# An adaLN block's forward and backward pass on one core: x in front of w_mod, the tail's loads and stores in a written order, and three filter gradients at a stage seam

## The chip, the core and the metric

The kernel runs on one core of a Trainium2 chip. The metric is the device time of one execution in microseconds. Three runs of the kernel before took 1512.26, 1512.44 and 1514.15; their median is 1512.44. The engines are named as in the profile: PE multiplies matrices (PEld loads its weights), DVE and ACT work on vectors, POOL and SP issue DMAs here, and POOL also does a few small vector operations. An engine executes its instructions in the order in which they stand in the program; PE, DVE, ACT, POOL and SP wait for each other through semaphores.

## What is computed

The reference is one block and its gradients. x is [1, 2048, 576], c is [1, 576], and the outputs are the block's result and eight gradients:

```
mod = (silu(c) @ w_mod).reshape(1, 6, 1, 576)        # sa, ca, ga, sb, cb, gb
h = layernorm(x) * (1 + ca) + sa
x = x + ga * irfft2(rfft2(h) * (w_r + 1j * w_i))     # spectral filter, 2048 x 576
h = layernorm(x) * (1 + cb) + sb
x = x + gb * ((h @ w_gate) * (h @ w_up) @ w_down)    # hidden width 4608
# returned: x, and the gradients of A_x, w_r, w_i, w_gate, w_up, w_down, c, w_mod
```

out_0 is the result, out_1 the gradient of x, out_2 and out_3 those of the filter (w_r, w_i), out_4 to out_6 those of the three big matrices, out_7 and out_8 those of c and w_mod.

## The kernel before

Rows are split into 16 tiles of 128 rows. The transforms are matmuls with tables of cosines and sines, made in steps over the 16 tiles and over 9 planes of frequencies (a plane and its mirror image are done as a pair, so there are 8 pairs). Three parts matter here.

**The head** (lines 330 to 640). SP issues the loads in a written order: c, a table, tile 0 of x (`x_load(0, 1)`, line 447), one section of w_mod (`mod_load(MGB)`), tiles 1 to 3 of x, four tiles of grad_out (gonA), w_down, tiles 4 to 7 of x, and so on. For each tile of x, `s1_stats` makes mean and variance on DVE (line 184) and ACT their root (186), `s1_norm` the normalized tile n1r (line 521, ACT, or 523, DVE), and `turn16` a first transform of it on PE into PSUM (line 200), which ACT copies out (203). `gate()` (line 504) multiplies the section of w_mod with silu(c) on PE and copies the result from PSUM to gbT on DVE (lines 512 and 516). `go_turn` transposes a tile of grad_out on PE (532) and scales it by gbT on DVE (533). Groups of the matmul u4 (576), which need four such tiles, are put between. A scheduler places the instructions of each engine by priority; `in_order` adds edges that fix an order on one engine.

**The middle** (lines 640 to 960) is one long PE-bound stretch over 36 blocks of the hidden width, from about 110 to 1235 us.

**The tail** (from line 960) is done in three stages and an end. Stage 1 (steps `t1_norm`, `t1_out`, `t1_turn`, one tile each, four steps deep) does the second layernorm's backward pass and stores gx1_d by POOL (line 1217). Stage 2 (`t2_cols`, `t2_rows`, `t2_filter`, `t2_back`, one pair of planes each) transforms and multiplies by the filter; `t2_more` makes the filter's gradients with `filter_grad(g)` (four DVE instructions, lines 1325 to 1327, and a load of Xn), those of even g one per step, and those of g = 3, 5 and 7 in the steps 4, 6 and 8. Stage 3 (`t3_cols`, `t3_rows`, `t3_norm`, `t3_sums`, one tile sa each) transforms back and does the first layernorm's backward pass: `t3_rows` multiplies on PE into one bank with the tag csB (line 282), ACT copies half of it to ye (284), and DVE folds both into ghr (285, 286) and so frees the bank; `t3_norm` loads gxc, makes gn (1426), w with its sum (1044), ab (1046) and u (1047), and in five tiles one more filter gradient; `t3_sums` makes ob (1052) in one of two buffers, and POOL stores it to out_1 (1464). POOL also halves two columns of the filter gradients (`scale_ends`, 1418), stores them in pieces of three planes (1439), and, at sa = 7, the mirrored planes to a scratch tensor gback_d (1443), from which SP copies them turned to out_2 and out_3 at the end (1531). At sa = 7 also four of the five loads of rows of w_mod's last four sections are issued (`section_load`), which `section_sum` (1157) sums on DVE at sa = 9, 10, 12, 13 and 14.

Beneath the three stages PE does the forward matmul of the block's second half as fill: 32 outputs n3, each of 36 matmuls u3p (line 1503), whose left operand comes in chunks `hl` of nine blocks through six slots, `hlt[0]` to `hlt[5]`, that lie over memory of earlier tiles; ACT copies a finished output (1508), DVE adds it to x1 (1516, 1517), and POOL stores it (1522). The first four chunks and the pieces of w_down are issued by POOL between the stores of gx1_d (`queued_load`), the later ones by SP. `deal` writes the order of PE, ACT and DVE for the whole tail by hand: so many fills to a step of each stage (24, 24, 26), then, at the end, 12 fills, a spread of dca (the gradient's row sums) on PE (1135), 12 fills, the spread of dsar, 80 fills, the last reduction gcp (1554), and the rest. Around the spreads ACT writes ten rows o8 of out_8 (1148); DVE sums five last sections, and makes gcd (1548) for gcp.

```
q = (0, 24, 24, 26)[stage]                       # line 1063
q = q * at // steps - q * (at - 1) // steps
...
hl = hlt[(0, 2, 3, 1, 4)[slot[0]] if slot[0] < 5 else (0, 2, 3, 5, 1, 4)[(slot[0] + 1) % 6]].tile(...)
...
if k in (4, 6, 8):
    filter_grad(k - 1)
```

The last tile pair takes its odd outputs (n3 = 29 and 31) in two banks, csA and csB, that hold sums of stage 3 before; csA is free once DVE has read dca and dsa from it (1121, 1127).

Of the kernel before, what the change touches and what calls it, by code (L numbers as in the profile page):

```python
# [19 lines left out]
NT = 16  # L20
# [66 lines left out]
def build(ctx, tc, A_x, A_w_r, A_w_i, B_w_gate, B_w_up, B_w_down, c_in, w_mod, grad_out,  # L87
# [240 lines left out]
    with ExitStack() as hs:  # L328
# [91 lines left out]
        def x_load(t0, t1):  # L420
            nc.sync.dma_start(h2p[:, t0:t1, 0:D], x_v[:, t0:t1, :])
# [23 lines left out]
        wms = {}  # L445
        T = {"F16": load_table(hp1, "F16")}
        x_load(0, 1)
        wms[MGB] = mod_load(MGB)
        x_load(1, 4)
        go_load(0)  # L450
        wd_load(0)
        x_load(4, 8)
# [129 lines left out]
        def u4_groups(n, eng=None):  # L582
            for _ in range(n):
                u4_group(u4_done[0], eng)
                u4_done[0] += 1

        gate()
        s1_norm(0)
        go_turn(0)
        s1_stats(1)  # L590
        s1_stats(2)
        for t in range(1, NT):
            if t in (3, 5, 7, 10):
                s1_stats({3: 4, 5: 6, 7: 8, 10: 12}[t])
            s1_norm(t)
            go_turn(t)
            if t == 1:
                pe_turn(0)
                wd_load(2)
                wms[MSB] = mod_load(MSB, True)  # L600
            if t == 2:
                mod_make(MGB, wms[MGB], "a")
                wms[MCB] = mod_load(MCB)
                for c, filt in enumerate((wr_v, wi_v)):
                    nc.sync.dma_start(back_d[c].rearrange("k j f -> j k f"), turned_rows(filt))
                nc.gpsimd.memset(wn[:, :, :, DF:FP], 0.0)
                for c, filt in enumerate((wr_v, wi_v)):
                    nc.sync.dma_start(wn[:, c, 0:NPR + 1, 0:DF], filt[:, 0:NPR + 1, :])
                    nc.sync.dma_start(wn[:, c, NPR + 1:NT, 0:DF], back_d[c])
                for k_ in ("GB", "I16"):  # L610
                    T[k_] = load_table(hp1, k_)
            if t == 3:
                pe_turn(1)
            if t == 7:
                scaled_table()
                mod_make(MCA, wms[MCA])
            if t == 11:
                shift_row()
                mod_make(MGA, wms[MGA], "a")
            if t == 14:  # L620
                mod_make(MSB, wms[MSB], "a")
            u4_groups({4: 2, 5: 1, 6: 1, 8: 2, 9: 1, 10: 1, 12: 2, 13: 1, 14: 1}.get(t, 0))
# [351 lines left out]
    with ExitStack() as ts:  # L974
# [79 lines left out]
        def deal(held, proj, ends):  # L1054
            made, s2, w2 = scaled["made"], scaled["2"], scaled["w2"]
            more, seq, acts = held + proj, list(lead), made[0:2] + s2[0:1] + w2[0:1] + made[2:3] + s2[1:2] + w2[1:2] + s2[2:3]
            dves, ofs = list(ends["sums"]), []
            for n, (stage, k, ins, own_a, own_v) in enumerate(staged):
                last_ = len(seq)
                seq += ins  # L1060
                steps = sum(x[:2] == (stage, k) for x in staged)
                at = sum(x[:2] == (stage, k) for x in staged[:n + 1])
                q = (0, 24, 24, 26)[stage]
                q = q * at // steps - q * (at - 1) // steps
                fills, more = more[:q], more[q:]
                seq += fills
                fill = [then_act[i_.name] for i_ in fills if i_.name in then_act]
                if stage == 1:
                    own = [then_act[i_.name] for i_ in ins if i_.name in then_act]
                    acts += own + s2[k + 1:k + 2] * (at == max(1, steps - 2) and k > 1) + (w2[k:k + 1] + made[k + 1:k + 2]) * (at == 1 and k > 1) + fill  # L1070
                else:
                    acts += own_a + fill
                    if at == 1:
                        now, ofs = ofs, []
                        if stage == 3:
                            dves += [i_ for nm, s_ in (("gn", 2), ("stt", 2), ("ob", 3), ("ab", 2), ("res", 2), ("fold", 1), ("unit", 2), ("sec", 2)) for i_ in ends["own"].get((nm, k - s_), [])]
                    if stage == 2:
                        dves += own_v
                    if at == steps:
                        dves += now  # L1080
                for i_ in fills:
                    ofs += then_dve.get(i_.name, [])
            dves += ofs + ends["dve"]
            sections, ofs = ends["sections"], []
            for at, ins, act in ends["pe"]:
                fills, more = more[:at], more[at:]
                seq += fills + ins
                acts += [then_act[i_.name] for i_ in fills if i_.name in then_act] + act
                ofs += [then_dve[i_.name] for i_ in fills if i_.name in then_dve]
            ofs += [then_dve[i_.name] for i_ in more if i_.name in then_dve]  # L1090
            cuts = (0, 2, 4, len(sections))
            for a, b, of in zip(cuts, cuts[1:], ([[]] * 3 + ofs)[-3:]):
                dves += sections[a:b] + of
            in_order(seq + more)
            in_order(acts)
            in_order(dves)
# [185 lines left out]
        def hl_load(nq, eng=nc.sync, behind_=None):  # L1282
            if nq >= 30:
                hl = new_wm()[:].rearrange("p (a b) -> p a b", b=256)
            else:
                slot[0] += 1
                hl = hlt[(0, 2, 3, 1, 4)[slot[0]] if slot[0] < 5 else (0, 2, 3, 5, 1, 4)[(slot[0] + 1) % 6]].tile([128, 9, 256], BF, name="hl")
            hl = hl if nq >= 30 else hl[:]
            queued(eng, behind_, hl, hhT_d[nq // 4, :, 9 * (nq % 4):9 * (nq % 4) + 9, :])
            if nq == 13:  # L1290
                in_order([last[eng], ld3["gxc", "ins", 0]])
            return hl
# [8 lines left out]
            return hl  # L1301

        first_hl = []
        for t, *loads in ((1, (0, 7), 0, (7, 7), (14, 7)), (2, 1), (3, (21, 7)), (4, 2), (5, (28, 7), (35, 1)), (6, 3)):
            for x in loads:
                if isinstance(x, int):
                    first_hl.append(queued_load(t, hl_load, x, nc.gpsimd))
# [21 lines left out]
        with ExitStack() as r2:  # L1329
# [18 lines left out]
            def t2_more(k):  # L1348
                if 1 < k < NPR + 2:
                    filter_grad(2 * pairs[k - 2])  # L1350
                if k in (4, 6, 8):
                    filter_grad(k - 1)
                if k in (1, 2):
                    spread((dcb, dga)[k - 1])
                if k == 2:
# [27 lines left out]

            def t2_back(n):
                plane_back(T["GB"], sds[n % 2], pairs[n], nrest, utB, new)

            pipeline(NPR, [t2_cols, t2_rows, t2_filter, t2_back], 2)
        T["IF"] = load_table(tl0, "IF", "tA", nc.gpsimd)
# [20 lines left out]
        def t3_rows(sa):  # L1409
            ye, *own["fold", sa] = rows_back(zzs[sa], [ps_fp.tile([128, 512], FP32, name="yp", tag="fp"), ps_cs.tile([128, 512], FP32, name="yp", tag="csB")], T["I16"][:], c3, ghr3[:, sa % 3, :])  # L1410
            own["ye", sa] = [ye]
            nc.sync.dma_start(xcs[sa % 3][:], x_v[:, sa, :])
            nc.scalar.activation(out=part(n1cs[sa % 3][:]), in_=part(xcs[sa % 3][:]), func=ACT.Identity, bias=nmr1g[:, sa:sa + 1], scale=rstd1g[:, sa:sa + 1])

        def scale_ends(s0, s1):
# [4 lines left out]
        def t3_norm(sa):  # L1420
# [15 lines left out]
                scale_ends(0, NPR + 1)  # L1436
            if sa > 3 and sa % 2 == 0:
                c, a = sa // 2 % 2, 3 * (sa // 4 - 1)
                nc.gpsimd.dma_start((o2_v, o3_v)[c][:, a:a + 3, :], wn[:, c, a:a + 3, 0:DF])
            if sa == 7:  # L1440
                scale_ends(NPR + 1, NT)
                for c in range(2):
                    nc.gpsimd.dma_start(gback_d[c], wn[:, c, NPR + 1:NT, 0:DF])
                rG.close()
                T["wm"] = pool("wme", 4)
                wmE.extend(section_load(m, MGA, 4, new_wm()) for m in range(4))
            if sa in (9, 10, 12, 13, 14):
                mark = traced()
                section_sum(len(own_e), wmE[len(own_e)][0], early, 4, 0)
                if not own_e:  # L1450
                    wmE.append(section_load(4, MGA, 4, new_wm()))
                own_e.append(sa)
                own["sec", sa] = of_engine(mark, "DVE")

        units, wmE, own_e = {0: 1, 1: 9, 3: 11, 4: 13, 6: 15}, [], []

# [3 lines left out]
        def t3_sums(sa):  # L1460
            ob = c3.tile([128, D], BF, name="ob1")
            ld3["last"] = norm_end(*ld3.pop(sa), n1cs[sa % 3][:], ob[:], "1").ins
            own["ob", sa] = [ld3["last"]]
            nc.gpsimd.dma_start(o1_v[:, sa, :], ob[:])
            if sa == 0:
                add_zero(csD, csE)
            diag(csD, csE, 0, ghr3[:, sa % 3, :], n1cs[sa % 3][:], DS, DC + 1, sa == NT - 1)

        pipeline(NT, [t3_cols, t3_rows, t3_norm, t3_sums], 3)
        mark = traced()  # L1470
        diag_rows(dca, csD, csE, 0, DC + 1)
        dsa = diag_sums(tl, csD, csE, 0, "dsa")
# [8 lines left out]
        for tp_ in range(NT // 2):  # L1481
# [10 lines left out]
            for group in [[(0, 0), (1, 0)], [(0, 1), (1, 1)]] if tp_ == 0 else [[(0, 0)], [(0, 1)], [(1, 0)], [(1, 1)]]:  # L1492
                mark = traced()
                p2 = {}
                for ti, h in group:
                    n3 = 4 * tp_ + 2 * ti + h
                    p2[ti] = ps_cs.tile([128, 512], FP32, name="u3q", tag="cs" + "AB"[n3 // 2 % 2]) if tp_ == NT // 2 - 1 and n3 % 2 else ps_u3.tile([128, 512], FP32, name="u3p")
                    if h == 0:
                        obs[ti] = o2p.tile([128, D], BF, name="ob3", bufs=3)
                mms = {}  # L1500
# [51 lines left out]
        for m0, w in ((0, 4), (4, 1)):  # L1552
# [3 lines left out]
                nc.scalar.copy(gcr[0:1, 0:512], pp[0:1, 0:512])  # L1556
            else:
                nc.vector.tensor_copy(gcr[0:1, 512:576], pp[0:1, 64:128])
        end_pe.append((80, pe_since(mark), of_engine(mark, "Activation")))
        nc.sync.dma_start(out_7[0:1, :], gcr[0:1, :])  # L1560
        in_order(end_sp)
        deal(held, proj, dict(sums=sums_dve, own=own, dve=end_dve, sections=sections, pe=end_pe))
# [58 lines left out]
```

## Time and profile before

| what | value |
|---|---|
| median of 3 runs | 1512.44 us (1512.26 to 1514.15) |
| the profiled execution | 1509.32 us |
| its span, first to last instruction | 1507.5 us |
| mean granted PE clock | 0.989 |
| PE idle, 0 to 20 us and 20 to 40 us | 7.6 and 1.8 us |
| PE idle, 1245 to 1305 us | 5.9 us |
| PE busy, 1355 to 1385 us | 23.8 of 30 us |
| PE busy, 1435 to 1455 us | 13.7 of 20 us |
| DVE busy, 1335 to 1385 us | 49.0 of 50 us |
| DMA share, 1325 to 1345 us; 1405 to 1465 us | 0.18 to 0.19; 0.91 to 1.09 |

The span runs from the first to the last instruction of one profiled execution; what the device time has more lies around it. A wait is given as the engine and line that waited, the engine or DMA that ended the wait, the total, how often, and the longest. In a timeline each row is a start, a duration, the engine, the line, the instruction with output<-inputs, and in brackets how long the engine stood idle before it and what ended that. Where the engine named had long been done, a DMA is the likelier cause.

### The profile page before, as it was taken

What the parts mean: (1) busy time and instruction counts of PE and PEld (TensorE: products, weight loads), DVE (VectorE), ACT (ScalarE), POOL (GpSimd) and SP (SyncE); (2) the same over time, 40 slices, a digit from 0 to 9 for tenths busy, and PEclk for the clock granted to TensorE, in tenths of its full rate; (3) what the DMA queues carried; (4) which work ended last, traced back from release to release, by engine and by line L of the source; (5) the groups of instructions that cost most, each with busy time, mean ns of one, the idle gap of its engine ahead of it and who ended that gap; (6) DMA issues with size and microseconds to landing.
All of it is one profiled execution on the core that took longest, in us unless ns stands there. A gap on an engine that the chain in (4) does not pass through costs nothing.

```text
span 1507.5 us, 27854 instructions
## 1 busy us (share of the span) xinstructions
PE 1460.3 (97%) x10713; PEld 987.2 (65%) x10713; DVE 1045.1 (69%) x2533; ACT 571.3 (38%) x1212; POOL 232.4 (15%) x368
## 2 busy tenths in 40 slices
PE   7999999999999999999999999999999998998986
PEld 5665544666666666666766766666666677776764
DVE  7485754666777776776766776677767667498876
ACT  6666733222222222222222222222222237575664
POOL 1101211110110110110211111111111122211311
PEclk8999999999999999999999999999999999999998
DMA  9867985888777778776876775876967769854894
GB/s 320 255 189 204 245 235 147 177 161 164 143 148 157 147 149 151 147 166 133 158 155 133 165 163 122 169 154 130 167 146 141 132 144 347 310 172 148 243 265 128
DMA packets 474404, 268.61 MB, mean 178 GB/s; under 512 B 397597, under 2 KB 444702, under 8 KB 473886
## 3 DMA queue, kind: packets, MB, share of 16 engines
q1 hardware_dynamic: 447246, 168.67, 52.5%
q0 software_dynamic: 27024, 98.16, 22.6%
q8 instruction: 84, 1.38, 0.4%
q14 instruction: 50, 0.41, 0.1%
HBM read 104.99 MB, written 78.89 MB: 122 GB/s over the span
## 4 chain that ended last, share of the span: by engine, by line
PE 83%; DVE 5%; DMA 4%; issue 4%; SPq 1%; ACT 1%; POOL 1%; POOLq 0%; DVEq 0%; ACTq 0%
PE u57p L785 26%; PE u8p L907 18%; PE gup L868 16%; PE u4p L576 9%; PE u3p L1503 3%; PE gup L863 3%; DMA out_dram<-ob 1%; PE fq L649 1%; DMA out_dram<-so 1%; DMA hl<-hhT_d 1%; DVE gwt L1325 1%; SPq L846 1%; PE fq L212 1%; PE fq L276 1%; PE fq L256 1%
## 5 line engine op out<-in xcount | busy, mean ns | idle before, releaser
L912 DVE TENSOR_TENSOR acc<-acc,u8p 128x288 f32<-128x288 f32 (+1 forms) x1088 | 483.0, 453 | 277.5 <-PE u8p L907 273.6
L907 PE MATMUL u8p<-wT,ggT 128*128 128x288 bf16 x1152 | 328.4, 287 | 1.5 <-DVE acc L912 1.4
L907 PE MATMUL u8p<-wT,guT 128*128 128x288 bf16 x1152 | 328.0, 286 | 0.0
L868 PE MATMUL gup<-h2T,wgu 128*128 128x512 bf16 x1152 | 297.9, 380 | 0.0
L787 ACT CAST so<-u57p 128x288 bf16<-128x288 f32 x208 | 82.7, 398 | 508.7 <-PE u57p L785 495.1
L785 PE MATMUL u57p<-h2p,gu_sf 128*128 128x288 bf16 x1088 | 176.7, 286 | 0.0
L785 PE MATMUL u57p<-h2p,gg_sf 128*128 128x288 bf16 x1088 | 176.7, 286 | 0.0
L868 PEld LDWEIGHTS <-wgu 128*128 128x128 bf16 x1152 | 109.6, 98 | 98.9 <-issue 18.1
L907 PEld LDWEIGHTS <-ggT 128*128 128x128 bf16 x1152 | 112.6, 98 | 66.5 <-issue 14.0
L576 PE MATMUL u4p<-goT,wdT 128*128 128x512 bf16 x668 | 154.6, 380 | 0.8 <-ACT ghh_st L172 0.8
L1503 PE MATMUL u3p<-wd,hl 128*128 128x288 bf16 x1044 | 147.0, 292 | 7.5 <-DMA hl<-hhT_d 4.5
L907 PEld LDWEIGHTS <-guT 128*128 128x128 bf16 x1152 | 112.7, 98 | 57.1 <-issue 2.0
L870 ACT CAST gT<-gup 128x512 bf16<-128x512 f32 x144 | 84.3, 585 | 131.4 <-PE gup L868 129.5
L1503 PEld LDWEIGHTS <-hl 128*128 128x128 bf16 x1080 | 105.4, 99 | 41.9 <-DMA hl<-hhT_d 6.0
L785 PEld LDWEIGHTS <-hh_sf 128*128 128x128 bf16 x1152 | 112.7, 98 | 28.4
L785 PEld LDWEIGHTS <-gu_sf 128*128 128x128 bf16 x1088 | 106.4, 98 | 27.0
L785 PEld LDWEIGHTS <-gg_sf 128*128 128x128 bf16 x1088 | 106.4, 98 | 26.8
L870 ACT CAST uT<-gup 128x512 bf16<-128x512 f32 x144 | 84.3, 585 | 77.9 <-PE gup L868 77.0
L576 PEld LDWEIGHTS <-wdT 128*128 128x128 bf16 x668 | 63.6, 98 | 72.2 <-issue 6.5
L785 PE MATMUL u57p<-gonC,hh_sf 128*128 128x288 bf16 x576 | 99.7, 286 | 0.0
L883 POOL DMA_DIRECT2D hhT_d<-hhT x36 | 33.2, 922 | 376.0 <-DVE hhT L872 352.9
L172 ACT CAST ghh_st<-u4p 128x512 bf16<-128x512 f32 x102 | 58.3, 585 | 59.7 <-PE u4p L576 57.9
(277 smaller groups left out, 1719.1 us busy)
## 6 DMA issues: line engine op xcount, KB each, us to landing
hhT_d<-hhT POOLq DMA_DIRECT2D x36, 512.0 KB, 6.4
ghhT_d<-ghh_st POOLq DMA_DIRECT2D x35, 512.0 KB, 4.1
ghh<-ghhT_d POOLq DMA_DIRECT2D x35, 512.0 KB, 7.8
hl<-hhT_d SPq DMA_DIRECT2D x26, 576.0 KB, 6.6
out_dram<-woT SPq DMA_DIRECT2D x68, 128.0 KB, 2.0
wd<-in_B_w_down_dram POOLq DMA_DIRECT2D x37, 144.0 KB, 4.1
wdn<-in_B_w_down_dram SPq DMA_DIRECT2D x18, 288.0 KB, 5.3
out_dram<-so SPq DMA_DIRECT2D x36, 144.0 KB, 2.9
```

What stands on the lines that cost most here:

```text
L172: nc.scalar.copy(dst, src)
L212: nc.tensor.matmul(p_[:, 0:FP], lhsT=G[:, k, pl, :], rhs=z, start=(n == 0), stop=(n == 1))
L576: nc.tensor.matmul(pt[:], lhsT=wdTs[k][:, j, m, :], rhs=goT[:, 4 * sb4:4 * sb4 + 4, m, :], start=(m == 0 and n == 5), stop=(m == n - 1))
L785: mm = nc.tensor.matmul(pw[0][:, 0:288], lhsT=sf[:, t, :], rhs=rhs_n(t, h * 288, 288), start=(t == 0), stop=(t == NT - 1))
L787: followed(mm, nc.scalar.copy(so[:, h * 288:(h + 1) * 288], pw[0][:, 0:288]))
L863: nc.tensor.matmul(pts[-1][:], lhsT=wgu[r, 8, jw * 128:(jw + 1) * 128], rhs=h2T[r, 4 * sb4:4 * sb4 + 4, 4, :], start=True, stop=False)
L868: nc.tensor.matmul(pts[k][:], lhsT=wgu[:, 4 * wi_ + m, jw * 128:(jw + 1) * 128], rhs=h2T[:, ts_, m, :], start=False, stop=(m == 3))
L870: nc.scalar.copy((gT, uT)[wi_][:, th_, :], pts[k][:])
L883: nc.gpsimd.dma_start(hhT_d[:, :, fb, :].rearrange("tp f x -> f tp x"), hhT[:].rearrange("f (tp ti) p -> f tp (ti p)", ti=2))
L907: nc.tensor.matmul(pu[:, 0:288], lhsT=l_, rhs=r_, start=(k == 0), stop=(k == len(mms) - 1))
L912: summed[t] = nc.vector.tensor_tensor(out=ghb(t)[:, hs_] if fbs[-1] == NFB - 1 else dst, in0=dst, in1=pu[:, 0:288], op=ADD).ins
L1503: mms[ti] = nc.tensor.matmul(p2[ti][:, 0:288], lhsT=hls[fb // 9][:, fb % 9, ti * 128:(ti + 1) * 128], rhs=w[:, fb - f0, h * 288:(h + 1) * ...
```

## The change

It has five parts. In the head, tile 1 of x is loaded before the section of w_mod, and an edge is written from the last of `gate()`'s DVE copies to the first DVE instruction of the statistics of tiles 4 and 5. In the first stage of the tail, the slots 2 and 3 of hl change places, and chunks 1 and 2 are queued behind stores 3 and 5 of gx1_d rather than 2 and 4. The filter gradients of g = 3, 5 and 7 move from the steps 4, 6 and 8 of stage 2 to behind the last `t2_back`. In stage 3 POOL's stores of filter gradients are each put behind a given ob store, gback_d is stored in two halves at sa = 9 and 13, and the five loads of w_mod are issued one per tile from sa = 7 to 11, each behind a given load of x (xc 11 to xc 15); a stage-3 step has 25 fills for 26. At the end only n3 = 31 takes a bank of the sums, and 100 fills stand ahead of gcp for 80.

```diff
         x_load(0, 1)
+        x_load(1, 2)
         wms[MGB] = mod_load(MGB)
-        x_load(1, 4)
+        x_load(2, 4)
...
+        mark = traced()
         gate()
+        gate_dve = on_dve(mark)[-1]
...
             if t in (3, 5, 7, 10):
+                mark = traced()
                 s1_stats({3: 4, 5: 6, 7: 8, 10: 12}[t])
+                if t == 3:
+                    in_order([gate_dve, on_dve(mark)[0]])
...
-                q = (0, 24, 24, 26)[stage]
+                q = (0, 24, 24, 25)[stage]
...
-                hl = hlt[(0, 2, 3, 1, 4)[slot[0]] if slot[0] < 5 else (0, 2, 3, 5, 1, 4)[(slot[0] + 1) % 6]].tile([128, 9, 256], BF, name="hl")
+                hl = hlt[(0, 3, 2, 1, 4)[slot[0]] if slot[0] < 5 else (0, 3, 2, 5, 1, 4)[(slot[0] + 1) % 6]].tile([128, 9, 256], BF, name="hl")
...
-        for t, *loads in ((1, (0, 7), 0, (7, 7), (14, 7)), (2, 1), (3, (21, 7)), (4, 2), (5, (28, 7), (35, 1)), (6, 3)):
+        for t, *loads in ((1, (0, 7), 0, (7, 7), (14, 7)), (3, (21, 7), 1), (5, 2, (28, 7), (35, 1)), (6, 3)):
...
-                if k in (4, 6, 8):
-                    filter_grad(k - 1)
...
             def t2_back(n):
                 plane_back(T["GB"], sds[n % 2], pairs[n], nrest, utB, new)
+                if n == NPR - 1:
+                    for g in (3, 5, 7):
+                        filter_grad(g)
...
-            nc.sync.dma_start(xcs[sa % 3][:], x_v[:, sa, :])
+            ld3["xc", sa] = nc.sync.dma_start(xcs[sa % 3][:], x_v[:, sa, :]).ins
...
             if sa > 3 and sa % 2 == 0:
                 c, a = sa // 2 % 2, 3 * (sa // 4 - 1)
-                nc.gpsimd.dma_start((o2_v, o3_v)[c][:, a:a + 3, :], wn[:, c, a:a + 3, 0:DF])
+                in_order([ld3["ob", sa - 1], nc.gpsimd.dma_start((o2_v, o3_v)[c][:, a:a + 3, :], wn[:, c, a:a + 3, 0:DF]).ins])
             if sa == 7:
                 scale_ends(NPR + 1, NT)
-                for c in range(2):
-                    nc.gpsimd.dma_start(gback_d[c], wn[:, c, NPR + 1:NT, 0:DF])
                 rG.close()
                 T["wm"] = pool("wme", 4)
-                wmE.extend(section_load(m, MGA, 4, new_wm()) for m in range(4))
+            if sa in (9, 13):
+                c = sa // 13
+                in_order([ld3["ob", sa - 1], nc.gpsimd.dma_start(gback_d[c], wn[:, c, NPR + 1:NT, 0:DF]).ins])
             if sa in (9, 10, 12, 13, 14):
...
-                if not own_e:
-                    wmE.append(section_load(4, MGA, 4, new_wm()))
...
+            if sa in range(7, 12):
+                wmE.append(section_load(sa - 7, MGA, 4, new_wm()))
...
-            nc.gpsimd.dma_start(o1_v[:, sa, :], ob[:])
+            ld3["ob", sa] = nc.gpsimd.dma_start(o1_v[:, sa, :], ob[:]).ins
...
+        in_order([i_ for m in range(5) for i_ in (ld3["xc", 11 + m], wmE[m][1])])
...
-                    p2[ti] = ps_cs.tile([128, 512], FP32, name="u3q", tag="cs" + "AB"[n3 // 2 % 2]) if tp_ == NT // 2 - 1 and n3 % 2 else ps_u3.tile([128, 512], FP32, name="u3p")
+                    p2[ti] = ps_cs.tile([128, 512], FP32, name="u3q", tag="cs" + "AB"[n3 // 2 % 2]) if n3 == 2 * NT - 1 else ps_u3.tile([128, 512], FP32, name="u3p")
...
-        end_pe.append((80, pe_since(mark), of_engine(mark, "Activation")))
+        end_pe.append((100, pe_since(mark), of_engine(mark, "Activation")))
```

## The prediction

> **What bounds the kernel now.** I read the busy row and the slices first, then who waited for whom in the last 270 us, then the timelines of the places that this names.
>
> ```profile
> span 1507.5 us, 27854 instructions
> PE 1460.3 (97%) x10713; PEld 987.2 (65%) x10713; DVE 1045.1 (69%) x2533; ACT 571.3 (38%) x1212; POOL 232.4 (15%) x368
> ...
> PE   7999999999999999999999999999999998998986
> ...
> PEclk8999999999999999999999999999999999999998
> ```
>
> PE is full for 1200 us; it idles in the first slice and the last eight, and only there can this change act. The waits of 1240 to 1508 us (total, times, longest):
>
> ```profile
> POOL hl L1273 <- DMA yc<-y_d: 8.2, 1, 8.2
> DVE ob L1052 <- DMA out_dram<-ob: 12.1, 3, 9.4
> PE yp L282 <- DVE ghr L286: 6.3, 1, 6.3
> PE fq L256 <- DVE sd L239: 4.4, 2, 2.2
> PE u3q L1503 <- DVE dsa L1127: 3.9, 1, 3.9
> PE gcp L1554 <- DVE gcd L1548: 3.7, 1, 3.7
> PE u3p L1503 <- ACT wo_l L820: 2.8, 1, 2.8
> PE fq L256 <- DVE sd L243: 1.6, 1, 1.6
> ```
>
> All but the 2.8 end on DVE, so DVE paces the tail. Its own long gaps, with what POOL and PE did at the second (start, duration, engine):
>
> ```profile
> 1390.80 0.46 DVE L285 TENSOR_TENSOR ghr<-yp,ye 128x289 bf16<-128x289 f32 x1 [5.07 <-ACT ye L284]
> ```
> ```profile
> 1434.72 1.00 POOL L1443 DMA_DIRECT2D gback_d<-wn  x1 [1.89 <-issue]
> 1435.50 1.33 POOL L1464 DMA_DIRECT2D out_dram<-ob  x2
> ```
> ```profile
> 1447.98 0.46 DVE L1052 TENSOR_TENSOR ob<-u,w 128x576 bf16<-128x576 bf16 x1 [9.44 <-DMA out_dram<-ob]
> ```
> ```profile
> 1449.67 0.42 PE L282 MATMUL yp<-zz,T_I 128*128 128x289 bf16 x1 [6.27 <-DVE ghr L286]
> ```
>
> Two ob stores sat on POOL behind both gback_d stores, whose doubling (L1418) had waited for a filter gradient. The store landed 12.4 us after its issue; DVE, with two ob buffers, stood 9.44 us, then PE.
>
> At the end everything hangs on T0 = 1483.77, when PE spreads dca: T0 to the span's end is 23.7 us. So the question is how much earlier DVE has dca.
>
> **The change, part by part.**
>
> *Head.* The stall to be attacked is PE's wait for gbT, whose copies stand on DVE behind statistics that wait for x(4,8):
>
> ```profile
> 15.04 0.82 DVE L184 BATCH_NORM_STATS2 ln_st<-h2p 128x6 f32<-128x288 bf16 x2 [1.39 <-DMA h2p<-in_A_x_dram]
> ```
> ```profile
> 16.10 0.29 PE L200 MATMUL tr<-T_F,n1r 128*128 128x128 bf16 x1 [2.37 <-DVE gbT L512]
> ```
> ```profile
> 23.78 0.45 PE L200 MATMUL tr<-T_F,n1r 128*128 128x128 bf16 x5 [1.79 <-ACT n1r L521]
> ```
>
> The new edge holds back only the first of tile 4's statistics. In the changed kernel's order the next two still stand ahead of the copies, with the same wait. So the 2.37 stays, and tile 1's earlier load only turns the 1.29 that PE waited for its n1r into more of the same wait. The extra SP issue (0.45) delays w_mod, which lies under a wait for gonA (1.48). But the order after the 23.78 row is new: ten u4 matmuls (2.32) and gonB's transposes now stand ahead of tr(4), where PE waited 1.79. n1r(5) then costs about 0.3 and the first of gonC's transposes are pulled forward 0.2: **1.5 gained**, between 0 (x lands 0.45 later and eats it) and 3.9 (1.5 plus 2.4, should the edge work). Later loads have margin: w_mod's MCA lands about 20 and is used at 30; wn is issued by 50 and used at 69.
>
> *First hl slots.* Chunk 1 took a slot that held yc until 1256.17, so POOL stood 8.2 us and gx stores 3 and 4 went out late; DVE then waited 2.12 for gx_d, ACT for DVE, PE 2.8 for wo_l. Chunk 1 now takes the slot over gonA (last read at 1246.0), behind gx 3 and wd(21,7): issued near 1252 instead of 1256. The 2.8 should go, but the DMA share is 1.03, 0.99 and 1.03 from 1245 to 1275, and chunk 3 landed just as PE wanted it (wait 0.28). **1.0 gained**, from -1 to 2.8.
>
> *Three filter gradients to the seam.* One is 2.31 us of DVE (two L1325 1.36, two L1326/7 about 0.9). In stage 2 DVE had no gap from 1340 to 1385, so the three removed (6.9) free the waits 2.15 + 2.21 + 1.64 = 6.0 of PE: without them PE reaches its last L256 at 1376.0, DVE its data at 1374.7. The three then run between the last product and the first fold. DVE's work to that point is unchanged, so DVE is free when it was, at 1385.65; the first ye, 6.0 earlier, is there at 1384.8. The fold moves from 1390.80 to 1385.65: **5.15 gained**, the gap being filled. From 4 (Xn loads, 2.8 us median landing, at two buffers) to 5.15.
>
> *Stage 3's stores and loads.* From fold 0 to dca DVE took 92.0 us: 77.0 of work and 15.0 of idle (0.95, 1.40, 2.10, 0.55, 9.44, 0.57). Work is the same, so a fold that starts earlier leaves idle alone to be argued. 0.95 and 0.57 are latencies to ACT, 0.5 of the 1.40 stays: 2.0 stays for sure. The 2.10, 0.55 and 9.44 are ob stores behind wn and gback_d stores; in the written order at most one such store stands between two ob stores, and doubling comes when its gradient is long done. What comes in their place: the five section loads are now issued one by one behind xc(11) to xc(15), about two steps (9 us) ahead of their sums, at a median landing of 6.0 (hl's longest: 12.6); and the stretch from 1380 to 1480 carried 81 us of transfers (56.0% + 25.4%), to be done now in some 87. I put 5 us of new DVE waits there, between 0 and 13: **8.0 gained** (13.0 down to 0). Fills fall from 26 to 25 a step: 19 matmuls of 0.1225, which PE does at the end. PE has 72 to 74 us of work against DVE's 77, so PE's own waits (2.11 for hl) are covered while they stay short of that.
>
> *The last bank (u3q for n3 = 31 alone), 100 fills.* The 3.93 for dsa goes, but PE meets T0 on DVE anyway: 0. After T0, n3 = 28's last matmul falls behind the spreads, so its ob copy stands on ACT behind ten o8 rows, ready at T0 + 9.3; n3 = 30 wants that bank at T0 + 6.3. PE waits 3.0, does 63 fills (7.7) and has gcp at T0 + 17.0 instead of 15.6 (gcd, by DVE, at 15.5). Behind gcp nine fills remain, and the 1.3 us by which ten ran slow after the 3.70 wait should go: -1.4 + 1.3 = -0.1. If the clock falls in the 3.0 wait as after the 2.84 at 1265.80 (15 matmuls took 3.59, 15 full-speed ones 2.00), -1.6. **-0.7 taken.**
>
> The Trainium skill, TensorE: Matmul & The Clock Gate, Part 1, has the clock halved only after an idle window of about 3.4 us. By it the 3.0 wait costs no clock and this term is -0.1; the slow 15 matmuls after 2.84 speak against it, and the sum would be 0.6 better.
>
> **Sum**: 1.5 + 1.0 + 5.15 + 8.0 - 0.7 = 15.0. The profiled execution took 1509.32 (span 1507.5 and 1.8 around it), so 1494.3 for its like. The median of the runs shown is 1512.44, 3.1 above it: **1497.4** forecast.
>
> **Rivals.**
> 1. *Transfers take the place of the order.* The DMA share was 0.91 to 1.05 in each ten us from 1425 to 1465 but one kind of store was late; if the share is the cause, ob stores and section loads stay late. Then 13.0 of idle stays: the sum is 1.5 + 1.0 + 5.15 - 0.7 = 7.0, so 1505.4. For: the ob store that took 12.4 us had four 576 KB section loads beside it. Against: it landed right behind the gback_d store issued before it (1434.72 + 12.7 = 1447.4), so queue order explains it. The Trainium skill, DMA: Bandwidth & Descriptors, Queues, rings and completion order, has each DMA engine round-robin between queues; by that SP's loads slow POOL's stores wherever they stand, which is this rival.
> 2. *Nothing comes back.* The 5 us of new waits are 0 and the clock holds: 20.6 gained, 1491.8. For: ob stores of quiet stretches landed in 4.8.
> 3. *Slower: just-in-time section loads.* Each of the five sums is in DVE's fixed order; a load later than its two steps stops DVE, and with it ACT's n1c, which releases the next xc and so the next section load on SP: the delay repeats. Break-even is at 20.0 (15.0 plus the 5 already counted) over five, 4.0 late each, a landing of 13 us. At the longest landing seen in this stretch (15.6, gxc), 6.6 late, five times 33: 13 slower, 1525. Against: 13 is rare beside a median of 5 to 6, and the second sum to the third has a spare step.
> 4. *The edge in the head does what it is called*: 2.4 more, 1495.0. The order speaks against it.
> 5. *No change* (within 0.2%, 3 us, about what a measurement of this kernel tells from none): rival 1 with the hl slots at -1 and two new late stores.
>
> **Chances.** Forecast (1493 to 1502, rival 4 with it) 0.58; rival 1 (1502 to 1509) 0.18; rival 2 (under 1493) 0.12; no change 0.05; slower, rival 3, 0.07. Faster 0.88. The range takes the forecast, most of rivals 1 and 2: 1490 to 1507.
>
> **What would show it.** Right: no L256 wait on sd; the first L285 about 5 us earlier against its stage; no ob wait over 3 us; T0 about 14 us earlier within the span, and 23.7 to 25 us from it to the end; a wait for gbT of 2 us or more still near 16 us; POOL without its 8.2. Wrong: section sums (L1157's line) that wait for wm; hl waits on PE over 3 us in stage 3; a yp wait on ghr that is not DVE's own work.

## The result, and the profile after

The changed kernel took 1495.11 us (median of 4, 1492.87 to 1496.36) against 1513.30 of the kernel before beside it: a ratio of 0.9878, 95% interval 0.9861 to 0.9895. The forecast was 1497.4, the range 1490 to 1507. A later comparison gave 1494.97 against 1508.66: 0.9910, 0.9894 to 0.9926. The changed kernel came out at the same time twice; the kernel before had medians of 1508.66 to 1513.30 in four comparisons, so the gain is 14 to 18 us. The profiled executions took 1509.32 and 1495.80: 13.5 less.

| point, us from the span's start | before | after |
|---|---|---|
| PE's wait for gbT in the head | 2.37 | 2.64 |
| PE's first stage-2 matmul (head done) | 56.47 | 57.20 |
| PE's waits for wo_l, then hl(3), 1260 to 1275 | 2.84, 0.28 | 0.17, 3.24 |
| PE's waits for sd (L256) in stage 2 | 6.0 | 1.5 |
| first fold of stage 3 (DVE L285), its wait | 1390.80, 5.07 | 1385.93, none |
| DVE idle from there to dca | 15.0 | 7.3 |
| T0, PE spreads dca | 1483.77 | 1470.45 |
| T0 to the span's end | 23.7 | 23.55 |

The page of the changed kernel, its span, busy row and slices of PE and of the granted clock:

```profile
span 1494.0 us, 27856 instructions
...
PE 1459.9 (98%) x10713; PEld 987.9 (66%) x10713; DVE 1045.2 (70%) x2533; ACT 570.5 (38%) x1212; POOL 232.6 (16%) x368
...
PE   7999999999999999999999999999999999899987
...
PEclk8999999999999999999999999999999999999989
```

Work is the same; what went is idle time in the last eight slices. What is left there shows in the waits from 1385 to 1475 us (total, times, longest):

```profile
PE u3p L1511 <- DMA hl<-hhT_d: 6.0, 2, 3.1
ACT ob L1516 <- PE u3p L1511: 5.8, 2, 5.5
DVE ab L1052 <- ACT u L1048: 5.2, 1, 5.2
...
DVE ob L1058 <- DMA out_dram<-ob: 1.1, 1, 1.1
```

The ob wait of 9.44 is gone, as forecast; so is every wait of PE on ghr. A wait stands there that was not named: DVE on ACT's u. The timelines of PE, ACT and DVE at that place (start, duration, engine, line):

```profile
1440.12 0.79 PE L1511 MATMUL u3p<-wd,hl 128*128 128x288 bf16 x5 [3.13 <-DMA hl<-hhT_d]
...
1445.82 0.90 PE L1511 MATMUL u3p<-wd,hl 128*128 128x288 bf16 x3 [2.87 <-DMA hl<-hhT_d]
```
```profile
1448.68 0.40 ACT L1516 CAST ob<-u3p 128x288 bf16<-128x288 f32 x1 [5.49 <-PE u3p L1511]
1448.98 0.78 ACT L1048 ACTIVATE u<-gn,rstd1g 128x576 bf16<-128x576 bf16 x1
```
```profile
1449.88 0.17 DVE L1052 TENSOR_SCALAR ab<-s 128x2 f32<-128x2 f32 x1 [5.22 <-ACT u L1048]
```

Read from the bottom: DVE lacks u; u stands in ACT's fixed order behind a copy of a fill's output; that output is late because its hl chunk is. A fill, which was there to use PE's spare time, thus stops DVE, the engine that sets the pace. The two waits for hl cost more than their 6.0: from 1440 to 1450 us PE's granted clock is 0.56, and the 12 matmuls at 1447.01 take 3.08 where 12 of the same shape take 1.63 at 1470.74.

### The profile page after: what moved, and what is told of

It reads as the page before. It is cut to its first block, busy times and chain, and to the rows that moved or that the text cites. A ratio compares the mean times of both kernels' runs of the same rounds, so it can differ in the third digit from the quotient of the medians.

```text
span 1494.0 us, 27856 instructions
## 1 busy us (share of the span) xinstructions
PE 1459.9 (98%) x10713; PEld 987.9 (66%) x10713; DVE 1045.2 (70%) x2533; ACT 570.5 (38%) x1212; POOL 232.6 (16%) x368
## 4 chain that ended last, share of the span: by engine, by line
PE 86%; DVE 5%; DMA 4%; ACT 2%; issue 2%; SPq 0%; POOL 0%; POOLq 0%; DVEq 0%; ACTq 0%
PE u57p L791 27%; PE u8p L913 19%; PE gup L874 17%; PE u4p L577 9%; PE u3p L1511 5%; PE gup L869 3%; DMA hl<-hhT_d 2%; PE fq L655 1%; PE fq L276 1%; PE fq L212 1%; PE fq L256 1%; DMA gx_d<-gxr 1%; DMA out_dram<-so 1%; DVE fm L231 1%; DVE gwt L1331 1%
## 5 line engine op out<-in xcount | busy, mean ns | idle before, releaser
L1511 PEld LDWEIGHTS <-hl 128*128 128x128 bf16 x1080 | 105.5, 99 | 44.1 <-DMA hl<-hhT_d 12.3
L876 ACT CAST uT<-gup 128x512 bf16<-128x512 f32 x144 | 84.3, 585 | 77.6 <-PE gup L874 77.6
```

Source lines behind the costliest of these rows:

```text
L876: nc.scalar.copy((gT, uT)[wi_][:, th_, :], pts[k][:])
L1511: mms[ti] = nc.tensor.matmul(p2[ti][:, 0:288], lhsT=hls[fb // 9][:, fb % 9, ti * 128:(ti + 1) * 128], rhs=w[:, fb - f0, h * 288:(h + 1) * ...
```

## The experiments

Eleven kernels were run, each beside the kernel before. Seven change one part of the changed kernel, one is that kernel again, three build on run 8.

**Run 1: the head as before.**

```
-x_load(1, 2)
 wms[MGB] = mod_load(MGB)
-x_load(2, 4)
+x_load(1, 4)
...
-in_order([gate_dve, on_dve(mark)[0]])
```

> The changed kernel with the head as it was: x(1,4) in one load behind w_mod, no edge. Read at the first stage-2 matmul of PE (fq L655 of the changed kernel, at 57.20 there, 56.47 before). Theory (the head's part of the change costs: w_mod lands a load later, and PE then waits for n1r and msl): the point returns to 56.5 +- 0.2, and the time is 0.7 less than the changed kernel's, about 1494.4, within what this can be told from. Rival (the 1.5 that was forecast is there and the 57.20 comes from the clock of one execution): the point stands at 57.9 to 58.7, the time about 1496.3.

1495.1 (1491.93 to 1497.41): the changed kernel's time. The first stage-2 matmul came at 56.23. But that point moves by itself: in the ten profiles with the changed head (that of the changed kernel and of runs 3 to 11) it lies between 55.06 and 57.73, mean 56.44; with the old head it is 56.47 and 56.23. So the 0.7 that the theory explained lies within that spread, and the rival's 1.5 is not there either: the head's part neither costs nor gains anything that these profiles can tell. The PE order that the prediction priced (ten u4 matmuls ahead of tr(4)) stands in this kernel too, so it isn't the head's edit that makes it; what it gains (PE's modc for MCA at 29.36, against 30.34 before) is down to 0.26 at the next modc (39.25 against 39.51), after a wait of 0.83 for n1r.

**Run 2: the edge on every statistic of tiles 4 and 5.**

```
-in_order([gate_dve, on_dve(mark)[0]])
+for i_ in on_dve(mark):
+    in_order([gate_dve, i_])
```

> The changed kernel with the edge on every statistic of tiles 4 and 5 and not the first alone. Theory (the prediction's reason why the wait stays: two statistics that wait for x(4,8) stand ahead of the gbT copies): PE's wait for gbT of 2.64 falls under 0.5, and the first stage-2 matmul comes 1.5 to 2.4 earlier, at 54.8 to 55.7; time about 1493. Rival 1 (gbT waits for w_mod's own products, not for the statistics): the wait stays over 2, the point at 57.2. Rival 2 (the statistics, now later, hold n1r(4) or msl, and the wait moves there): gbT's wait goes, but the point stays at 56.8 to 57.4.

1496.82 (1494.5 to 1499.6). PE's timeline in the head:

```profile
16.32 2.60 PE L402 MATMUL modps<-wm,sc_rep 128*128 128x288 bf16 x10
...
29.24 0.59 PE L200 MATMUL tr<-T_F,n1r 128*128 128x128 bf16 x5 [1.55 <-ACT n1r L522]
29.63 1.07 PE L417 MATMUL modc<-sc_bf,wm 128*128 128x1 bf16 x25
30.63 2.58 PE L402 MATMUL modps<-wm,sc_rep 128*128 128x288 bf16 x10
```

The wait for gbT is gone, so the reading of the order was right: PE is at modps at 16.32 instead of 18.59. At 30.6 nothing of it is left, and the first stage-2 matmul comes at 58.42, not at the 54.8 to 55.7 of the theory and later than in any other run. Rival 2 was right that the wait moves: PE now waits for n1r (0.26 and 1.55), and behind that it runs at a granted clock of 0.50 from 30 to 36 us (the ten modps take 2.58 instead of 1.40). Its reason, that the later statistics make n1r late, isn't shown: the last n1r of this stretch ends at 29.2 us, against 29.4 in the changed kernel. n1r came hardly earlier, while PE did. The prediction's rival 4 is out.

**Run 3: the three filter gradients back in steps 4, 6 and 8.**

```
+if k in (4, 6, 8):
+    filter_grad(k - 1)
...
-if n == NPR - 1:
-    for g in (3, 5, 7):
-        filter_grad(g)
```

> The changed kernel with the three filter gradients back in steps 4, 6 and 8 of stage 2. Theory (the term of 5.15): PE waits again for sd, 5 to 6 in all, the first fold goes from 1385.9 to about 1390.8, T0 and the end move by the same: 5 slower than the changed kernel, about 1500.1. Rival (PE or a transfer catches up in stage 3, since its 5.22 wait on ACT u comes from hl loads and not from DVE): the first fold is 5 later, but the wait on u falls by as much, and the time is 1495 to 1497.

1503.38 (1500.0 to 1505.73), 8.4 above the changed kernel, more than either expectation. Waits for sd are back (2.16, 0.72, 3.31 at the three places), the first fold waits 4.95 again, and two waits for ACT follow it (0.83, 1.40), which the changed kernel has not.

**Run 4: the third stage's stores and loads as before**, that is the written order taken out, both gback stores and four section loads at step 7.

```
-in_order([ld3["ob", sa - 1], nc.gpsimd.dma_start((o2_v, o3_v)[c]...
+nc.gpsimd.dma_start((o2_v, o3_v)[c]...
 if sa == 7:
+    for c in range(2):
+        nc.gpsimd.dma_start(gback_d[c], wn[:, c, NPR + 1:NT, 0:DF])
...
+    wmE.extend(section_load(m, MGA, 4, new_wm()) for m in range(4))
-if sa in (9, 13):
...
```

> The changed kernel with the tail's third stage as it was: both gback stores and four section loads at its step 7, no order between the stores. Theory (the term of 8.0, of which the changed kernel's profile bears out 7.7): ob waits for its store 9 to 12 us again, T0 lies 7 to 8 later after the first fold: about 1503. Rival 1 (the transfers are the cause, the order is nothing): the time stays within 2 of the changed kernel's 1495.1. Rival 2 (the 5.22 wait on u belongs to the new order, and goes with it): DVE's idle between first fold and dca is 13 to 15 in all as before, no u wait, 1503; that the hl waits of PE (3.13 and 2.87 in the changed kernel) are gone then shows that they came with the new places of the loads.

1500.87 (1498.44 to 1502.09): 5.9 slower than the changed kernel, not 8. DVE idles 12.9 from the first fold to dca, against 7.3; two ob waits are nearly all of it:

```profile
1404.64 0.46 DVE L1058 TENSOR_TENSOR ob<-u,w 128x576 bf16<-128x576 bf16 x1 [3.62 <-DMA out_dram<-ob]
1440.23 0.46 DVE L1058 TENSOR_TENSOR ob<-u,w 128x576 bf16<-128x576 bf16 x1 [8.66 <-DMA out_dram<-ob]
```

On POOL's queue the ob store of 1395.72 stands behind three stores of filter gradients and lands after 8.8 us, and the two of 1427.81 and 1428.89 stand behind a gback_d store and land after 12.4. The wait for u and the late hl loads are gone with the new order, as rival 2 said: the changed kernel exchanged 12.3 of ob waits for 1.1 of them and 5.6 of others.

**Run 5: the changed kernel again**, beside runs 6 to 8.

> The changed kernel once more, as it is, beside the next three, so that they have a neighbour: its head, its last bank and its hl waits are the same code as in the first four runs. Theory (the clock after the wait for the ob copy of n3 = 28 depends on how much PE idled just before): after that wait of 2.73 the 18 matmuls take 3.7 to 4.0 instead of 2.37 where PE waited over 1.5 at T0, and T0 to the end is 25.2; they take 2.37 and 23.5 where it waited 1.0 or less, as in the first profile of this kernel. Rival (by the wait alone): 2.37 after 2.73 each time. In the head, first stage-2 matmul at 56.3 to 57.2. Time 1493 to 1497.

1494.97 (1492.99 to 1496.27). T0 waited 1.52; after the 2.72 the first 18 matmuls took 3.33 and the next 18 3.12, instead of 2.37 each, and T0 to the end was 25.3. The first 18 lost less than the theory's 3.7 to 4.0, both together lost the 1.7 that it takes to come to 25.2; the last section has all seven executions with that wait. The first stage-2 matmul came at 55.06, earlier than the 56.3 that was expected.

**Run 6: the hl slots and their load order as before.**

```
-(0, 3, 2, 1, 4) ... (0, 3, 2, 5, 1, 4)
+(0, 2, 3, 1, 4) ... (0, 2, 3, 5, 1, 4)
-(3, (21, 7), 1), (5, 2, (28, 7), (35, 1)), (6, 3)
+(2, 1), (3, (21, 7)), (4, 2), (5, (28, 7), (35, 1)), (6, 3)
```

> The changed kernel with the hl slots and the order of the first hl loads as before. Only POOL's queue between 1240 and 1290 differs. Theory (the term of 1.0): POOL waits 8 again for a slot, PE waits 2.8 for wo_l, but the wait of 3.2 that hl(3) has in the changed kernel is gone: the stage-3 transposes of the tail's first stage (the tr that lies at 1285 to 1288) come later by 0 to 1.5 and the time is 1.0 up, 1496. Rival (2.8 gained, as the wait for wo_l alone says): 2.8 up, 1498. Rival (one wait in place of the other): 0.

1494.65 (1493.27 to 1496.16), no difference, as the rival with 0 said. PE's timeline, this run first, the changed kernel second:

```profile
1264.96 3.46 PE L1511 MATMUL u3p<-wd,hl 128*128 128x288 bf16 x15 [2.93 <-ACT wo_l L826]
1274.13 2.87 PE L1511 MATMUL u3p<-wd,hl 128*128 128x288 bf16 x22 [0.71 <-DMA hl<-hhT_d]
```
```profile
1273.76 4.54 PE L1511 MATMUL u3p<-wd,hl 128*128 128x288 bf16 x22 [3.24 <-DMA hl<-hhT_d]
```

One wait in place of the other, and each slows the matmuls behind it (15 in 3.46 instead of 2.00; 22 in 4.54 instead of 2.87).

**Run 7: the last bank and the fills as before** (u3q for n3 = 29 and 31, 26 fills a step, 80 at the end).

```
-q = (0, 24, 24, 25)[stage]
+q = (0, 24, 24, 26)[stage]
...
-... if n3 == 2 * NT - 1 else ps_u3...
+... if tp_ == NT // 2 - 1 and n3 % 2 else ps_u3...
...
-end_pe.append((100, ...
+end_pe.append((80, ...
```

> The changed kernel with u3q for n3 = 29 and 31, 26 fills a step and 80 at the end, as before. Theory (the term of -0.1 to -1.6 for the end): PE waits about 4 for dsa and 1 to 3.7 for gcp, no ob wait of 2.7; T0 to the end 23.7 as before the change, so 1.5 less than in the runs where the clock fell in the 2.73 and 0.2 more than where it didn't: time 1494 to 1495.5. Rival (the fills, 26 instead of 25, take PE's place in stage 3): T0 comes up to 2 later, 1497.

1498.77 (1495.62 to 1515.52): 3.8 slower. Behind T0 it is no worse (23.2 to the end). The loss is ahead of T0, on PE's timeline:

```profile
1446.12 1.14 PE L1511 MATMUL u3p<-wd,hl 128*128 128x288 bf16 x4 [7.48 <-DMA hl<-hhT_d]
```

With 26 fills a step PE comes to the chunk earlier, the chunk comes no earlier, and yp behind it makes DVE's fold wait 6.64. The rival named the place; the price is larger.

**Run 8: the gback stores at steps 13 and 15.**

```
-if sa in (9, 13):
-    c = sa // 13
+if sa in (13, 15):
+    c = sa // 15
```

> The changed kernel with its two gback stores at steps 13 and 15 of the third stage instead of 9 and 13: the one of 1430 goes to about 1457, out of the stretch 1425 to 1450, where the DMA share is 0.95 to 1.05 and hl and wm loads took 10 to 13 instead of 5 to 7. Theory (the DMA share makes the hl loads late; PE's two hl waits of 3.1 and 2.9 hold ACT's ob copy, which stands ahead of u, and so DVE 5.2): the two hl waits sum to under 4, DVE's longest wait for u falls under 3, T0 comes 2 to 4 earlier, time 1491 to 1493. Rival (hl is late because wm loads stand ahead of it on the same queue): hl waits and the wait for u as they are, time as the changed kernel's. Rival (the store, put later, holds the last ob stores or the gback copy at the end): slower by 1 to 4.

1488.52 (1486.46 to 1492.35), ratio 0.9873, 0.9854 to 0.9893, 6.5 below the changed kernel beside it. PE's hl waits in stage 3 fell from 6.0 to 1.4, DVE's wait for u is gone, and DVE has only 0.57 of idle from the first fold to dca, T0 77.6 behind the fold instead of 84.5. The two queues (packets, MB, share of the DMA engines) and the DMA issues (KB each, median us from issue to landing) between 1425 and 1450 us, changed kernel first:

```profile
q1 hardware_dynamic: 2158, 5.35, 70.8%
q0 software_dynamic: 695, 2.36, 29.6%
...
hl<-hhT_d SPq DMA_DIRECT2D x4, 576.0 KB, 10.0
wm<-in_w_mod_dram SPq DMA_DIRECT2D x3, 576.0 KB, 8.6
...
gback_d<-wn POOLq DMA_DIRECT2D x1, 505.8 KB, 11.2
```
```profile
q1 hardware_dynamic: 2697, 6.86, 81.6%
q0 software_dynamic: 554, 1.83, 18.5%
...
hl<-hhT_d SPq DMA_DIRECT2D x4, 576.0 KB, 6.4
wm<-in_w_mod_dram SPq DMA_DIRECT2D x3, 576.0 KB, 6.6
```

q0 is POOL's queue, q1 SP's. SP's order is the same in both, so the store on POOL's queue made SP's loads late: hl by 3.6 (the one load, issued at 1430, whose landing is known), wm by 2.0, and xc and gxc by 5.6 and 6.4 (11.7 against 6.1, 12.8 against 6.4). The shares of the two queues sum to about 1.0 in either kernel; what differs is who has them. 0.53 MB on POOL's queue took 11.1% of the engines' time, and without them SP's queue moved 1.51 MB more in 10.8%. The Trainium skill, DMA: Bandwidth & Descriptors, Queues, rings and completion order, says that each DMA engine goes round between the queues that have work for it, a packet at a time. The trace agrees in so far as loads of one queue came late beside a store on the other; the turns themselves it doesn't show. Here that was 6.5 us of the kernel's time.

The stores were now issued at 1451.87 and 1461.81. The share is high there too (0.97 from 1445 to 1465 us), but the last load of a chunk is issued at 1447.6.

**Run 9: run 8, and u3q for n3 = 30 too.**

```
-tag="cs" + "AB"[n3 // 2 % 2]) if n3 == 2 * NT - 1 else
+tag="cs" + "AB"[n3 % 2]) if n3 >= 2 * NT - 2 else
```

> The kernel with the gback stores at steps 13 and 15, and u3q (a bank that dca's sums leave) for n3 = 30 too, not for 31 alone. Theory (the 2.7 that n3 = 30 waits for the ob copy of 28, with the clock it costs in most executions, is on the path until gcp): the wait goes, PE comes to gcp at T0 + 14.4 instead of 17.1 and waits about 1 there for gcd, T0 to the end falls from 25.1 to 22 to 22.5: 2.5 to 3 less than the kernel with late gback stores, about 1485.7. Rival (gcd, from DVE behind o8's sections, is the bound): T0 to the end 24 or more, within 1 of it.

1488.06 (1486.76 to 1490.06), ratio 0.9855, 0.9840 to 0.9870: the fastest, though not told from run 8. The wait of 2.7 went, but T0 itself waited 3.69 for dca, and the 12 matmuls behind it took 3.08 instead of 1.63: gcp came at T0 + 17.1 and not 14.4, and T0 to the end was 23.4. That is neither the theory's 22 to 22.5 nor the rival's 24; the time is the rival's (within 1 of run 8), but not for its reason, since PE didn't wait for gcd. Nothing tells that the bank gained: run 11, which has it for n3 = 31 alone, gets to gcp at T0 + 17.25 behind a like wait (4.16).

**Run 10: run 8 with the filter gradients back in steps 4, 6 and 8** (edit of run 3).

> The kernel with the gback stores at steps 13 and 15, and the three filter gradients back in steps 4, 6 and 8 of stage 2, so that the third stage has no hl wait of its own that could hide or double the price. Theory A (the prediction's term): the first fold 5.15 later, everything behind it the same: 1493.7. Theory B (what the same edit did with the early gback stores): the first fold 5 later, and the two waits for ACT right behind it (0.8 and 1.4) come with it, since they too are PE's lateness: 7 to 7.5 later, 1495.7. Rival (in the third stage the lateness is caught up, since PE has less work than DVE there): under 3 later, 1491.

1497.45 (1496.65 to 1504.79), 8.9 above run 8, in the profiled executions 6.0. There T0 comes 7.5 later, as theory B says: 5.0 at the first fold and 2.5 behind it. T0 to the end is 23.5, against 25.1 in run 8, and so the end hides 1.5 of it. DVE's timeline at the seam:

```profile
1391.37 0.46 DVE L285 TENSOR_TENSOR ghr<-yp,ye 128x289 bf16<-128x289 f32 x1 [6.62 <-ACT ye L284]
1394.44 0.17 DVE L1052 TENSOR_SCALAR ab<-s 128x2 f32<-128x2 f32 x1 [0.83 <-ACT u L1048]
1396.37 0.46 DVE L285 TENSOR_TENSOR ghr<-yp,ye 128x289 bf16<-128x289 f32 x1 [1.40 <-ACT ye L284]
```

**Run 11: run 8 with four section loads at once at step 7** and the fifth behind the first sum, as before the change.

> The kernel with the gback stores at steps 13 and 15, and the section loads as before the change: four at once at step 7, the fifth behind the first sum; the stores keep their written order. It parts the two halves of the stage-3 edit. Theory (the stores are what stopped DVE, the loads had margin): ob waits stay under 2, DVE's idle between the first fold and dca stays under 2, time within 1 of the kernel with late gback stores, 1487.5 to 1489.5. Rival (four section loads at once put hl and ob late): hl waits or ob waits of 2 to 5, and the time up by as much.

1490.86 (1490.41 to 1491.78), ratio 0.9873 as in run 8, and 2.8 above run 9 beside it. DVE idles 2.95 from the first fold to dca, in ob waits of 1.48 and 1.47, where run 8 has 0.57; hl waits are 0.7. The theory had said under 2, and a time of 1487.5 to 1489.5: this is the rival's price, at its lower end, by ob. No section sum waited for its load. So the order of the stores is most of the stage-3 edit, and that of the loads 3 us at most.

## Why the prediction was right, point by point

The sum held (15.0 forecast; 13.5 in the profiled executions, 14 to 18 in the medians), but not term by term: three terms were too high (head, hl slots, stage 3), one was too low (filter gradients), and one that was put at nothing wasn't (the fills). That these cancel is luck.

- **Head, 1.5: nothing.** Failed step: "n1r(5) then costs about 0.3". The fill did cover the 1.79, PE was ahead at 30 us, and n1r took back most of it; and the order that was priced isn't the head edit's (run 1). That the edge does not work, and why, was right (run 2); that it would be worth 2.4 if it did was wrong: its gain goes to n1r and to the clock.
- **hl slots, 1.0: nothing** (run 6). The 2.8 went as said. But chunk 3, which "landed just as PE wanted it", was then wanted 3.7 earlier (1270.52 for 1274.26) and landed only 0.8 earlier (1273.76 for 1274.54). The two waits cancel.
- **Filter gradients, 5.15: 6 to 9** (runs 3, 10). The mechanism was right, the size was the cap that DVE's own work sets (fold at 1385.65 forecast, 1385.93 measured). Not every wait for sd went: 1.5 of the 6.0 stayed, where none was forecast. The failed step is "2.0 stays for sure": the 0.95 and the 1.40 behind the first fold were no latencies but the rest of PE's lateness. Both are gone in the changed kernel and back in runs 3 and 10 (0.83, 1.40).
- **Stage 3, 8.0: 5.9** (run 4). The ob waits fell to 1.1, as said. New waits of 5.6 (5.22 and 0.39) stand beside it. That is near the "5 us of new DVE waits", but by luck, for they don't stand at the section loads: no sum waited for one, neither one by one nor all at once (run 11). They came by hl, PE and ACT, and that is the failed step. It goes back to the list of waits, which ends in "All but the 2.8 end on DVE" but leaves out a row of the same view, on which this could have been seen:

```profile
PE u3p L1503 <- DMA hl<-hhT_d: 4.5, 4, 2.1
```

  The text then had PE's 2.11 for hl "covered" by DVE's longer work. PE's time was; ACT's order, in which u stands behind the fill's copy, is not in its sum. Of the prediction's own signs of being wrong, "hl waits on PE over 3 us in stage 3" came, with 3.13. Rival 1 was thus half of the truth: queue order made ob late, and the gback_d store's part of the DMA engines then made hl late. The first is shown by run 4 (which undoes the loads' order too, worth 3 at most by run 11), the second by run 8. With both out of the way the edit is worth 12.3 (run 4 against run 8, medians of two comparisons; DVE's idle says the same, 12.9 against 0.57).
- **Fills 26 to 25: not counted, part of 3.8** (run 7). They were put down as matmuls "which PE does at the end". They also set when PE asks for hl, and DVE hangs on that through ACT. How much of the 3.8 is theirs and how much the bank's wasn't measured apart; the 7.48 wait lies before any instruction that the bank changes.
- **End, -0.7.** The wait of 3.0 for the ob copy was 2.73, gcp came at T0 + 17.1 (17.0 forecast), the clock cost 0 in two executions and 1.7 in five: T0 to the end is 23.6 there and 25.1 to 25.3 here, close to the two ends of the term (-0.1 and -1.6; by the prediction's own rows the lower end is -1.7, the 1.6 of the slow 15 on top of the -0.1).
- **Rival 3** (slower by section loads) did not come: no sum waited.

The single undoings add up to 17.9 (0.1 and 8.4 and 5.9 and -0.3 and 3.8, each against 1494.97), more than the 13.7 of the comparison that 1494.97 comes from. Runs 3, 4 and 7 each change the same hl waits in stage 3 (5.3, 0 and 7.5 instead of 6.0), so their prices overlap; by how much wasn't measured.

## What to carry to other kernels

When a stall goes, ask of each engine's written order what stands ahead of the pace-setter's next input: here a copy for fill work stood ahead of it, so a late load of the fill stopped the whole chain. Ordering a store on its queue cures the queue, not the share of the DMA engines that it takes from loads on another queue; put it where no load that the chain waits for stands beside it, as run 8 did. And price a stall that is removed with the small waits right behind it: they are often its tail, not latencies of their own.

## What the runs showed of the hardware

Short waits cost clock at some times and not at others. After the same wait of 2.72 or 2.73 for the ob copy, the 18 matmuls ran at a granted clock of 1.00 in one execution (changed kernel), and at 0.63 and then 0.53 in another (run 8):

```profile
1479.87 2.37 PE L1511 MATMUL u3p<-wd,hl 128*128 128x288 bf16 x18 [2.73 <-ACT ob L1516]
```
```profile
1473.35 4.04 PE L1511 MATMUL u3p<-wd,hl 128*128 128x288 bf16 x18 [2.72 <-ACT ob L1516]
```

In seven executions with that wait, the two whose wait at T0, nine us before, was 1.01 and 1.26 kept the speed; the five with 1.52, 1.61, 1.69, 1.95 and 2.33 lost 1.7 (gcp at T0 + 18.8 instead of 17.1). In runs 4, 9, 10 and 11, whose wait at T0 was 3.19 to 4.16, the speed was lost right behind T0: 12 matmuls in 2.85 to 3.08 instead of 1.63. That is a regularity of a few rows, not a cause shown. The Trainium skill, TensorE: Matmul & The Clock Gate, Part 1, puts the fall of the clock at an idle window of about 3.4 us; these rows disagree in so far as a single wait of 2.7, and in run 2 one of 1.55, was followed by it.
